# Batch 0 of a blockwise causal attention in two query parts, with the MoE layer begun between them

## The chip, the cores and the metric

The kernel runs on one core of a Trainium2 chip. The metric is the device time of one execution in microseconds (us), as a median over runs. Engine names: PE is TensorE (matmuls; PEld its weight loads), DVE is VectorE, ACT is ScalarE, POOL is GpSimd, SP is SyncE, which only issues DMAs here.

## The reference: what is computed

Attention over 8 batches, 8 heads, 576 positions and a head dimension of 64, with a mask that is causal by blocks of 64, followed by a maxout layer over all 4608 tokens.

```python
scores = scale * np.matmul(q, k.transpose(0, 1, 3, 2))        # (8, 8, 576, 576)
mask = block_i >= block_j                                     # blocks of 64
scores = np.where(mask, scores, -1000000000.0)
scores = scores - np.max(scores, axis=-1, keepdims=True)
attn = np.exp(scores)
attn = attn / (np.sum(attn, axis=-1, keepdims=True) + 1e-09)
attn_out = np.matmul(attn, v)
...
x = attn_out.transpose(0, 2, 1, 3).reshape(B * S, H * D)      # (4608, 512)
h1 = x @ w1                                                   # w1, w2: (512, 1024)
h2 = x @ w2
return np.maximum(h1, h2) @ w_out                             # w_out: (1024, 512)
```

All inputs and the output are float32; the kernel's matmuls take bf16.

## The kernel before, in words

The program is one straight stream for each engine; the order in which the Python code issues instructions is the order in which every engine runs its own, since the scheduler is set to manual. Waits between engines come from the tiles' dependencies.

**Attention.** Work goes by pairs of heads: 32 pairs (`p` or `s`), four to a batch, two to a group (`g`). A group's q and k come by DMA as float32 (`load_qk`, SP's queue, 576 KB each), are cast to bf16 (`cast`, on POOL, ACT or DVE), and turned on the PE by 18 small transposes each (`transposes`, L265), which ACT and DVE copy from PSUM to `qT` and `kT` (L272). `scores` (L282) makes the transposed scores of a pair: keys on partitions, queries along the free axis. They are issued in two bursts, `burst_a` and `burst_b`, through two PSUM buffers (`ps_s`); ACT's exponential (L288) writes them to `aT`: three of 1024 elements (512 columns of two heads) and one of 128. POOL's `mask` (L293) sets half blocks on the diagonal to zero. `av` (L333) multiplies with v, whose 65th column of ones gives the sum; 30 matmuls of 65 columns for a pair, for query tiles [0, 1] and [2, 3, 4]. DVE takes the reciprocal and multiplies (L339, L340) into `xp`; after a group, `x_out` turns it on the PE (18 small transposes) and DVE copies it into `xT` (L358, L359), the MoE layer's input with the model dimension on partitions. `done_tokens` is raised once both groups of a batch are there.

**MoE.** `h_unit(i, f)` takes one span of 512 tokens and one slice of 128 of the hidden dimension: 4 matmuls (L168) with w1, 4 with w2; DVE copies the first to bf16 (L175) and takes the maximum with the second (L177). `y_unit(i, s)` makes 128 rows of the output with 8 matmuls (L186), which ACT copies (L192) and SP stores. `y_last` does the last 128 rows in halves. Each matmul is one step of a generator, `moe()`; `needs` lists for each step how many tokens must be done; `ready()` counts the steps that may go, and `fill(n)` issues up to n of them at the place where it is called. `fill_of(s)` sets n: what is ready less 6, over the pairs left until the next batch is done.

**PSUM.** `ps_s` has two buffers of two banks; everything else on the PE takes one of four banks (`ps_m`).

**Order of the head.** `warm_up(n)` issues n matmuls on zeros (L254). q and k of the groups 0 to 2 are loaded at once, those of group 3 and 4 later (`pool_work`, each behind a small POOL memset that gates SP's DMA). POOL's queue also issues v (`load_v`, L109, five chunks for a batch), w1 and w2 (`load_w`, L120: columns 0 to 255, 256 to 511, then 512 to 1023) and w_out (`load_wo`, L123), all of them with a cast in the DMA; these use eight semaphores in turn, so that an issue waits for the landing of the one eight places earlier. After the four pairs of batch 0 come their `av`, the two `x_out`, and from there a loop over the pairs 4 to 31: a fill, `burst_a`, a fill, the transposes of a later group's q or k, `burst_b`, POOL's work, and the `av` of two pairs earlier with fills between. At pair 4 the transposes of group 2 (q and k) come first, between two fills of 6.

Of the kernel before, what the change touches and what calls it, by code (L numbers as in the profile page):

```python
# [14 lines left out]
def kernel(  # L15
# [38 lines left out]

    SPAN = 512
    NSPAN = NTOK // SPAN

# [31 lines left out]
    def load_qk(g, queues, gated=False):  # L89
        b, u = divmod(g, GPB)  # L90
        for nm, src, queue in (("q", q, queues[0]), ("k", k, queues[1])):
            raws[nm, g] = t = raw.tile([P, 2, RPP * D], FP32, name=f"{nm}raw")
            if gated:
                nc.gpsimd.memset(t[:, 0, :1], 0.0)
            queue.dma_start(
                out=t[:],
                in_=src[b, 4 * u:4 * u + 4].rearrange(
                    "(s h) (p t) d -> (h p) s (t d)", h=2, t=RPP),
            )
# [35 lines left out]
    load_qk(2, (SP, SP))  # L135
# [9 lines left out]
    cast("q", 0, ((dve, 0, 6), (pool, 6, RPP)))  # L145
# [3 lines left out]
    cast("q", 1, ((pool, 0, RPP),))  # L149
    for c in range(3, NCH):  # L150
        load_v(0, c)
    load_w(0, 256)
    load_w(256, 256)
# [5 lines left out]
    def h_unit(i, f):  # L159
# [3 lines left out]
        t0 = i * SPAN  # L163
        ph = []
        for w_sb in (w1_sb, w2_sb):
            pt = ps_m.tile([P, SPAN], FP32, name="ps_h", tag="m")
            for c in range(NDM):
                nc.tensor.matmul(  # L168
                    pt[:], w_sb[:, c, f * P:(f + 1) * P], xT[:, c, t0:t0 + SPAN],
                    start=(c == 0), stop=(c == NDM - 1),  # L170
                )
                if c == NDM - 1:
                    if not ph:
                        h1 = h1_pool.tile([P, SPAN], BF16, name="h1")
                        nc.vector.tensor_copy(out=h1[:], in_=pt[:])  # L175
                    else:
                        nc.vector.tensor_max(g[:, f, :], h1[:], pt[:])  # L177
# [3 lines left out]
    def y_unit(i, s):  # L181
        g = g_tiles[i]
        t0 = i * SPAN + s * P
# [12 lines left out]
    def y_last(i, s):  # L196
        g = g_tiles[i]
        t0 = i * SPAN + s * P
# [17 lines left out]
    def moe():  # L216
        ny = SPAN // P
        for i in range(NSPAN):
            need = (i + 1) * SPAN
            for f in range(NFF):  # L220
                yield from ((need, 0) for _ in h_unit(i, f))
                if i > 1 and f % 2 == 0:
                    yield from ((need, 0) for _ in y_unit(i - 1, f // 2))
            if i == 0:
                for s in range(ny):
                    yield from ((need, 0) for _ in y_unit(0, s))
        for s in range(ny - 1):
            yield from ((NTOK, 0) for _ in y_unit(NSPAN - 1, s))
        yield from ((NTOK, 0) for _ in y_last(NSPAN - 1, ny - 1))


    needs = []
    for i in range(NSPAN):
        needs += [(i + 1) * SPAN] * (2 * NDM * NFF + (SPAN // P * NFF if i != 1 else 0))
    needs += [NTOK] * ((SPAN // P + 1) * NFF)
    moe_steps = moe()
    at = [0]

    def ready():
        n = at[0]  # L240
        while n < len(needs) and needs[n] <= done_tokens[0]:
            n += 1
        return n - at[0]

    def fill(n):
        for _ in range(min(n, ready())):
            next(moe_steps)
# [44 lines left out]
    def mask(p, a0):  # L292
        nc.gpsimd.memset(aT_r[p % NA][BLK:, :, a0:a0 + BLK], 0.0)  # L293
# [23 lines left out]
    def av(p, ts):  # L317
# [11 lines left out]
        for gi, t in enumerate(ts):  # L329
            for hh in range(2):  # L330
                for c in range(t + 1):
                    a0 = CB[c] + t * P
# [12 lines left out]
    def x_out(g):  # L345
        b, u = divmod(g, GPB)
        xp = xps.pop(g)
        pe = ps_m.tile([P, 2, NCH, BLK], BF16, name="ps_xe", tag="m")
        po = ps_m.tile([P, 2, NCH - 1, BLK], BF16, name="ps_xo", tag="m")
        for s in range(2):  # L350
            for t in range(NCH):
                src = xp[:, t, s].rearrange("p a d -> p (a d)")
                nc.tensor.transpose(pe[:, s, t, :], src[:BLK], ident[:BLK, :BLK])  # L353
                if t < NCH - 1:
                    nc.tensor.transpose(po[:, s, t, :], src[BLK:], ident[BLK:, BLK:])
        dst = xT[:, 2 * u:2 * u + 2, b * S:b * S + NCH * P].rearrange(
            "p s (t h w) -> p s t h w", h=2, w=BLK)
        nc.vector.tensor_copy(out=dst[:, :, :, 0], in_=pe[:])  # L358
        nc.vector.tensor_copy(out=dst[:, :, :NCH - 1, 1], in_=po[:])  # L359
        if u == GPB - 1:  # L360
            done_tokens[0] = (b + 1) * S
# [13 lines left out]
    def pool_work(s):  # L375
        g, i = divmod(s, 2)
        if s == 0:
            load_w(512, 512)
            load_qk(3, (SP, SP), gated=True)
        elif s == 1 or s == 2:  # L380
            pass
        elif s == 3:
            cast("q", 2, ((act, 0, RPP),))
# [146 lines left out]
```

The softmax here doesn't subtract the row's maximum and nothing guards it: scores larger than these inputs give would overflow.

## Time and profile before

| | |
|---|---|
| median of 7 runs | 294.15 us (293.81 to 296.1) |
| profiled execution | 294.15 us, span from first to last instruction 292.4 us |
| granted PE clock | 1.00 |
| PE busy | 277.1 us, of which MoE h 133.6, MoE y 66.5 |
| DVE, ACT, POOL busy | 182.2, 140.1, 95.1 us |
| matmuls on zeros | 34 recorded, 10.9 us busy |
| first MoE matmul | recorded at 27.2 us, the following four at 28.19 |
| first scores of pair 4 and pair 5 | 32.14 and 36.75 us |
| exponentials of batch 0 | 9.32 to 22.5 us |

How to read it: times are from the start of the span; a row of the timeline gives start, length, engine, line, operation, output and inputs, and in brackets the idle time just before and what ended it. Matmuls overlap in their pipeline: a single one of 512 columns lasts 379 ns, and in a stream one starts every 217 ns (92 in 20 us between 240 and 260 us). A row "x4" is several instructions merged from the first start to the last end. The landing of a DMA is counted from its issue.

### The profile page before, as it was taken

What the parts mean: (1) busy time and instruction counts of PE and PEld (TensorE: products, weight loads), DVE (VectorE), ACT (ScalarE), POOL (GpSimd) and SP (SyncE); (2) the same over time, 40 slices, a digit from 0 to 9 for tenths busy, and PEclk for the clock granted to TensorE, in tenths of its full rate; (3) what the DMA queues carried; (4) which work ended last, traced back from release to release, by engine and by line L of the source; (5) the groups of instructions that cost most, each with busy time, mean ns of one, the idle gap of its engine ahead of it and who ended that gap; (6) DMA issues with size and microseconds to landing.
All of it is one profiled execution on the core that took longest, in us unless ns stands there. A gap on an engine that the chain in (4) does not pass through costs nothing.

```text
span 292.4 us, 7406 instructions
## 1 busy us (share of the span) xinstructions
PE 277.1 (95%) x3067; PEld 141.1 (48%) x3116; DVE 182.2 (62%) x363; ACT 140.1 (48%) x200; POOL 95.1 (33%) x236
## 2 busy tenths in 40 slices
PE   8787999999999999999999999999999999999995
PEld 3345445445554454544554455454545544444443
DVE  6717677547987676666565666666665766464530
ACT  3883687686655555554545555545555000101112
POOL 3958336625644443144324432443111000000000
PEclk9999999999999999999999999999999999999999
DMA  7999998959923792668656684455110111011104
GB/s 269 284 206 285 218 183 163 234 139 178 201 25 149 91 218 45 201 73 203 80 200 72 167 117 151 73 63 66 40 38 37 38 67 43 36 72 38 72 36 144
DMA packets 56081, 36.65 MB, mean 125 GB/s; under 512 B 38768, under 2 KB 43376, under 8 KB 56048
## 3 DMA queue, kind: packets, MB, share of 16 engines
q0 software_dynamic: 41728, 7.87, 33.6%
q1 hardware_dynamic: 13760, 27.60, 27.7%
q10 hardware_dynamic: 560, 0.72, 0.7%
q8 instruction: 24, 0.39, 0.6%
q14 instruction: 9, 0.07, 0.1%
HBM read 34.60 MB, written 9.44 MB: 151 GB/s over the span
## 4 chain that ended last, share of the span: by engine, by line
PE 90%; ACT 4%; DVE 3%; issue 2%; ACTq 0%
PE ps_h L168 42%; PE ps_y L186 20%; PE ps_o L333 11%; PE ps_s L282 8%; ACT aT L288 3%; PE ps_w L254 3%; PE ps_qT L265 2%; PE ps_kT L265 2%; PE ps_xe L353 2%; DVE xp L340 1%; PE ps_y L203 1%; DVE kT L272 1%; DVE xT L358 0%; DVE qT L272 0%; DVE rec L339 0%
## 5 line engine op out<-in xcount | busy, mean ns | idle before, releaser
L168 PE MATMUL ps_h<-xT,w_sb 128*128 128x512 bf16 x547 | 133.6, 379 | 3.5 <-issue 1.8
L288 ACT ACTIVATE aT<-ps_s 128x1024 bf16<-128x1024 f32 (+1 forms) x128 | 99.1, 832 | 53.6 <-PE ps_s L282 53.6
L168 PEld LDWEIGHTS <-w_sb 128*128 128x128 bf16 x576 | 51.9, 98 | 59.7 <-issue 6.1
L175 DVE CAST h<-ps_h 128x512 bf16<-128x512 f32 x72 | 49.7, 691 | 45.0 <-PE ps_h L168 43.8
L186 PE MATMUL ps_y<-wo_sb,g 128*128 128x512 bf16 x262 | 66.5, 379 | 1.0 <-issue 0.2
L293 POOL MEMSET aT<- 64x128 bf16 x128 | 23.5, 199 | 123.0 <-ACT aT L288 122.8
L192 ACT COPY y<-ps_y 128x512 f32<-128x512 f32 x35 | 20.5, 586 | 83.9 <-PE ps_y L186 56.8
L177 DVE TENSOR_TENSOR g<-h,ps_h 128x512 bf16<-128x512 bf16 x72 | 49.3, 684 | 10.2 <-PE ps_h L168 10.2
L333 PEld LDWEIGHTS <-aT 128*128 128x128 bf16 x960 | 33.6, 98 | 15.0 <-DVE xp L340 8.5
L333 PE MATMUL ps_o<-vv,aT 128*128 128x65 bf16 x960 | 39.7, 194 | 1.1 <-DVE xp L340 0.4
L186 PEld LDWEIGHTS <-g 128*128 128x128 bf16 x280 | 25.4, 98 | 27.9 <-issue 3.2
L282 PE MATMUL ps_s<-qT,kT 64*128 64x64 bf16 (+4 forms) x384 | 34.4, 275 | 3.3 <-ACT aT L288 3.2
L109 POOL DMA_DIRECT2D vv<-in_v_dram x40 | 33.7, 849 | 0.3 <-issue 0.3
L340 DVE TENSOR_TENSOR xp<-ps_o,rec 128x256 bf16<-128x256 f32 x64 | 31.4, 491 | 2.2
L282 PEld LDWEIGHTS <-kT 64*128 64x128 bf16 x384 | 16.5, 94 | 18.9 <-issue 13.1
L339 DVE RECIPROCAL rec<-ps_o 128x4 f32<-128x4 f32 x64 | 11.8, 184 | 18.9 <-PE ps_o L333 18.8
L105 POOL CAST qn<-qraw 128x1152 bf16<-128x1152 f32 (+1 forms) x15 | 16.7, 1111 | 4.3 <-DMA qraw<-in_q_dram 4.3
L272 DVE COPY qT<-ps_qT 128x576 bf16<-128x576 bf16 x17 | 12.8, 757 | 5.8 <-PE ps_qT L265 4.5
L358 DVE COPY xT<-ps_xe 128x640 bf16<-128x640 bf16 x16 | 7.8, 490 | 12.4 <-PE ps_xe L353 12.1
L272 DVE COPY kT<-ps_kT 128x576 bf16<-128x576 bf16 x17 | 12.8, 756 | 4.3 <-PE ps_kT L265 3.3
L105 POOL CAST kn<-kraw 128x1152 bf16<-128x1152 f32 x13 | 14.9, 1146 | 0.8
L254 PE MATMUL ps_w<-zeros 128*128 128x512 bf16 x34 | 10.9, 454 | 1.8 <-DVE zeros L132 1.2
(39 smaller groups left out, 103.3 us busy)
## 6 DMA issues: line engine op xcount, KB each, us to landing
qraw<-in_q_dram SPq DMA_DIRECT2D x16, 576.0 KB, 4.5
out_dram<-y SPq DMA_DIRECT2D x35, 256.0 KB, 2.1
kraw<-in_k_dram SPq DMA_DIRECT2D x15, 576.0 KB, 5.6
vv<-in_v_dram POOLq DMA_DIRECT2D x32, 128.0 KB, 5.8
w_sb<-in_moe_w_dram POOLq DMA_DIRECT2D x4, 256.0 KB, 9.0
w_sb<-in_moe_w_dram POOLq DMA_DIRECT2D x2, 512.0 KB, 16.8
wo_sb<-in_moe_w_out_dram POOLq DMA_DIRECT2D x2, 512.0 KB, 12.7
kraw<-in_k_dram ACTq DMA_DIRECT2D x1, 576.0 KB, 5.3
```

The costliest lines, as they stand in the source:

```text
L105: copy(out=n[:, j0:j1], in_=t[:, j0:j1])
L109: nc.gpsimd.dma_start(out=vv_r[b % NV][:rows, c, :, :D], in_=v[b, :, c * P:c * P + rows, :].rearrange("h p d -> p h d"),)
L168: nc.tensor.matmul(pt[:], w_sb[:, c, f * P:(f + 1) * P], xT[:, c, t0:t0 + SPAN], start=(c == 0), stop=(c == NDM - 1),)
L175: nc.vector.tensor_copy(out=h1[:], in_=pt[:])
L177: nc.vector.tensor_max(g[:, f, :], h1[:], pt[:])
L186: nc.tensor.matmul(py[:], g[:, f, s * P:(s + 1) * P], wo_sb[:, f, :], start=(f == 0), stop=(f == NFF - 1),)
L272: copies[i](out=t[:, :S].rearrange("q (p j) -> q p j", j=RPP), in_=pts[i].rearrange("q j p -> q p j"),)
L282: nc.tensor.matmul(ps[:m, hh, col:col + w], kT[r, c * P:c * P + m], qT[r, q0:q0 + w], start=True, stop=True,)
L288: nc.scalar.activation(out=aT_r[p % NA][:m, :, a0:a0 + w], in_=ps[:m, :, :w], func=AF.Exp, scale=scale,)
L293: nc.gpsimd.memset(aT_r[p % NA][BLK:, :, a0:a0 + BLK], 0.0)
L333: nc.tensor.matmul(po[:, gi, hh, :], a[:, hh, a0:a0 + P], vv[:, c, h0 + 2 * hh, :], start=(mm == 0), stop=(mm == n_mm - 1),)
L340: nc.vector.tensor_mul(xp[:, ts[0]:ts[0] + n, :, p % 2], po[:, :, :, :D], rec[:, :n].to_broadcast([P, n, 2, D]),)
```

## The change

Batch 0's queries are cut at position 384. For the four pairs of batch 0 the scores of the first 384 queries come first, in bursts of 512 and 256 columns (`burst_p1`, `burst_p2`); then those of the last 192, in bursts of 512 and 320 (`burst_q1`, `burst_q2`). So the four exponentials of a pair have 1024, 512, 1024 and 640 elements. `a_col` finds a block's place in `aT` for these pairs. `av` is called for the query tiles [0, 1, 2] and [3, 4], `x_out` for the tiles 0 to 2 and 3 to 4; `done_tokens` becomes 384 after the first part of group 1.

The first MoE span of 512 tokens becomes two, of 384 and 128. `fill` and `ready` count cost in place of steps: a step of 384 columns is 0.75, one of 128 is 0.25. The y units of spans 0 and 1 follow the h units of span 1.

In the head: q0's cast is split 7 to 2 between DVE and POOL; q1 is cast by DVE and k1 by POOL (before, the other way round). k2's load is issued later, behind a POOL memset that follows the first `load_w`. The masks of pairs 2 and 3 in the first part go to DVE. The first `load_w` comes behind pair 0's masks and ahead of v's chunks 3 and 4. q2 and k2 are cast by POOL in place of ACT, and their transposes come within batch 0, with all four copies on DVE. The casts of q3 and k3 on POOL stand behind both issues of w_out, before they stood between v's chunks 2 and 3 of batch 1. The matmuls on zeros are 37 (before 36), at other places. The first two `fill`s of 6 at pair 4 are gone; 17 steps of the 384-token span are issued before the loop, and the `av` for the tiles 3 and 4 of the pairs 2 and 3 in the loop at pair 4.

```diff
+    QCUT = 384
+    def a_col(p, c, t):
+        if p >= HP:
+            return CB[c] + t * P
+        return {
+            0: (0, 768 - QCUT), 1: (512 - P, 960 - QCUT),
+            2: (384 - 2 * P, 1152 - QCUT), 3: (0, 1344 - QCUT), 4: (0, 1536 - 4 * P),
+        }[c][t * P >= QCUT] + t * P if (c, t) != (2, 4) else 1280
     SPAN = 512
-    NSPAN = NTOK // SPAN
+    spans = [(0, QCUT), (QCUT, SPAN - QCUT)]
+    spans += [(t0, SPAN) for t0 in range(SPAN, NTOK, SPAN)]
+    NSPAN = len(spans)
...
-    load_qk(2, (SP, SP))
+    load_qk(2, (SP, None))
...
-    cast("q", 0, ((dve, 0, 6), (pool, 6, RPP)))
+    cast("q", 0, ((dve, 0, 7), (pool, 7, RPP)))
     cast("k", 0, ((act, 0, 5), (dve, 5, RPP)))
     for c in range(3):
         load_v(0, c)
-    cast("q", 1, ((pool, 0, RPP),))
-    for c in range(3, NCH):
-        load_v(0, c)
-    load_w(0, 256)
-    load_w(256, 256)
+    cast("k", 1, ((pool, 0, RPP),))
...
-        t0 = i * SPAN
+        t0, w = spans[i]
...
-                    pt[:], w_sb[:, c, f * P:(f + 1) * P], xT[:, c, t0:t0 + SPAN],
+                    pt[:, :w], w_sb[:, c, f * P:(f + 1) * P], xT[:, c, t0:t0 + w],
...
+    def plan():
+        def h(i, f):
+            t0, w = spans[i]
+            units.append((h_unit(i, f), t0 + w, w / SPAN, 2 * NDM))
+        def y(i, s, last=False):
+            t0, w = spans[i]
+            if last:
+                units.append((y_last(i, s), t0 + w, 0.5, 2 * NFF))
+            else:
+                units.append((y_unit(i, s), t0 + w, 1.0, NFF))
         for i in range(NSPAN):
-            need = (i + 1) * SPAN
             for f in range(NFF):
-                yield from ((need, 0) for _ in h_unit(i, f))
-                if i > 1 and f % 2 == 0:
-                    yield from ((need, 0) for _ in y_unit(i - 1, f // 2))
-            if i == 0:
-                for s in range(ny):
-                    yield from ((need, 0) for _ in y_unit(0, s))
-        for s in range(ny - 1):
-            yield from ((NTOK, 0) for _ in y_unit(NSPAN - 1, s))
-        yield from ((NTOK, 0) for _ in y_last(NSPAN - 1, ny - 1))
-    needs = []
-    for i in range(NSPAN):
-        needs += [(i + 1) * SPAN] * (2 * NDM * NFF + (SPAN // P * NFF if i != 1 else 0))
-    needs += [NTOK] * ((SPAN // P + 1) * NFF)
-    moe_steps = moe()
+                h(i, f)
+                if i > 2 and f % 2 == 0:
+                    y(i - 1, f // 2)
+            if i == 1:
+                for j in range(2):
+                    for s in range(spans[j][1] // P):
+                        y(j, s)
+        n = spans[-1][1] // P
+        for s in range(n):
+            y(NSPAN - 1, s, s == n - 1)
+    plan()
...
+        n, total = at[0], 0.0
+        while n < len(steps) and steps[n][1] <= done_tokens[0]:
+            total += steps[n][2]
             n += 1
-        return n - at[0]
+        return int(total)
     def fill(n):
-        for _ in range(min(n, ready())):
-            next(moe_steps)
+        while n > 0 and at[0] < len(steps) and steps[at[0]][1] <= done_tokens[0]:
+            u, _, cost = steps[at[0]]
+            next(u)
+            n -= cost
...
+    def burst(p, parts, a0):
+        u = ps_s.tile([P, 2, 512], FP32, name="ps_s", tag="s")
+        w = 0
+        for c, q0, n in parts:
+            scores(p, u, w, c, q0, n)
+            w += n
+        exp(p, u, w, a0)
+    def burst_p1(p):
+        burst(p, ((0, 0, QCUT), (2, 256, P)), 0)
+    def burst_p2(p):
+        burst(p, ((1, P, QCUT - P),), 512)
+    def burst_q1(p):
+        burst(p, ((0, QCUT, 192), (1, QCUT, 192), (2, QCUT, P)), 768)
+    def burst_q2(p):
+        burst(p, ((2, 512, BLK), (3, QCUT, 192), (4, 512, BLK)), 1280)
+    def masks_p(p, eng=None):
+        for a in (0, 384, 512):
+            mask(p, a, eng)
+    def mask_q(p, eng=None):
+        mask(p, 1344, eng)
...
-                    a0 = CB[c] + t * P
+                    a0 = a_col(p, c, t)
...
-            done_tokens[0] = (b + 1) * S
+            done_tokens[0] = min(b * S + t1 * P, (b + 1) * S)
...
-        if s == 0:
-            load_w(512, 512)
-            load_qk(3, (SP, SP), gated=True)
-        elif s == 1 or s == 2:
-            pass
-        elif s == 3:
-            cast("q", 2, ((act, 0, RPP),))
-            cast("k", 2, ((act, 0, RPP),))
-            load_qk(4, (SP, SP), gated=True)
-            for c in range(3):
-                load_v(1, c)
-            cast("q", 3, ((pool, 0, RPP),))
-            cast("k", 3, ((pool, 0, RPP),))
-            for c in range(3, NCH):
-                load_v(1, c)
-            load_wo(0, 4)
-            load_wo(4, 4)
-        elif s == 4:
+        if s == 4:
...
-    for s in range(HP):
-        burst_a(s)
-        if s == 0:
-            cast("k", 1, ((dve, 0, RPP),))
-            warm_up(4)
-        elif s == 1:
-            transposes("k", 1, (dve, dve))()
-            warm_up(2)
-        elif s == 2:
-            av(0, [0, 1])
-            warm_up(2)
-        else:
-            av(0, [2, 3, 4])
-        burst_b(s)
-        pool_work(s)
-        if s == 0:
-            transposes("q", 1, (dve, dve))()
-            warm_up(2)
-        elif s == 1:
-            warm_up(4)
-        elif s == 2:
-            warm_up(3)
-    for p in (1, 2, 3):
-        av(p, [0, 1])
-        av(p, [2, 3, 4])
-        if p == 2:
-            x_out(0)
-    x_out(1)
+    cast("q", 1, ((dve, 0, RPP),))
+    burst_p1(0)
+    burst_p2(0)
+    warm_up(2)
+    masks_p(0)
+    load_w(0, 256)
+    load_qk(2, (None, SP), gated=True)
+    cq = transposes("q", 1, (dve, dve))
+    burst_p1(1)
+    ck = transposes("k", 1, (dve, dve))
+    for i in range(2):
+        cq((i,))
+        ck((i,))
+    burst_p2(1)
+    masks_p(1)
+    for c in range(3, NCH):
+        load_v(0, c)
+    warm_up(2)
+    burst_p1(2)
+    warm_up(2)
+    av(0, [0, 1, 2])
+    burst_p2(2)
+    masks_p(2, nc.vector)
+    load_w(256, 256)
+    warm_up(3)
+    burst_p1(3)
+    av(1, [0, 1, 2])
+    warm_up(2)
+    burst_p2(3)
+    masks_p(3, nc.vector)
+    load_w(512, 512)
+    load_qk(3, (SP, SP), gated=True)
+    cast("q", 2, ((pool, 0, RPP),))
+    cast("k", 2, ((pool, 0, RPP),))
+    burst_q1(0)
+    av(2, [0, 1, 2])
+    warm_up(2)
+    burst_q2(0)
+    av(3, [0, 1, 2])
+    x_out(0, 0, 3)
+    burst_q1(1)
+    warm_up(2)
+    burst_q2(1)
+    mask_q(0)
+    mask_q(1)
+    for c in range(3):
+        load_v(1, c)
+    warm_up(3)
+    burst_q1(2)
+    x_out(1, 0, 3)
+    fill(4)
+    burst_q2(2)
+    mask_q(2)
+    fill(2)
+    burst_q1(3)
+    av(0, [3, 4])
+    fill(3)
+    burst_q2(3)
+    cq = transposes("q", 2, (dve, dve))
+    ck = transposes("k", 2, (dve, dve))
+    for i in range(2):
+        cq((i,))
+        ck((i,))
+    mask_q(3)
+    for c in range(3, NCH):
+        load_v(1, c)
+    load_wo(0, 4)
+    load_wo(4, 4)
+    load_qk(4, (SP, SP), gated=True)
+    cast("q", 3, ((pool, 0, RPP),))
+    cast("k", 3, ((pool, 0, RPP),))
+    av(1, [3, 4])
+    fill(3)
+    x_out(0, 3, NCH)
     x_due = []
     for s in range(HP, NPAIR):
         g, i = divmod(s, 2)
         if x_due:
-            x_out(x_due.pop())
+            x_out(x_due.pop(), 3 if s == HP + 1 else 0)
         n = fill_of(s)
-        if s == HP:
-            fill(6)
-            cq = transposes("q", 2, (dve, act))
-            ck = transposes("k", 2, (dve, act))
-            cq()
-            ck()
-            fill(6)
         burst_a(s)
         n_a = n // 2 if n > 12 else n * 2 // 5
         n_b = n // 6
...
             av(p, [2, 3, 4])
             if p % 2:
                 x_due.append(p // 2)
+        elif s == HP:
+            av(2, [3, 4])
+            fill(n_b)
+            av(3, [3, 4])
+            x_due.append(1)
```

The lines left out hand the widths to the other MoE operations, put `x_out`'s tile range into its slices, build `steps` from `plan()` in place of `moe()`, and rename `needs`.

## The prediction

> **What bounds the kernel now.** I read the page first (busy shares, groups), then the busy time by stage, then TensorE's timeline, then ScalarE, GpSimd and the DMA issues of the stage that the change touches.
>
> ```profile
> PE 277.1 (95%) x3067; PEld 141.1 (48%) x3116; DVE 182.2 (62%) x363; ACT 140.1 (48%) x200; POOL 95.1 (33%) x236
> L168 PE MATMUL ps_h<-xT,w_sb 128*128 128x512 bf16 x547 | 133.6, 379 | 3.5 <-issue 1.8
> ```
>
> TensorE is busy for 95% of the span, and of the idle time almost none lies before MoE matmuls. But the share counts the matmuls on zeros (L254), and it is an average. By stage:
>
> ```profile
> 6.94:28.19 21.25, 16.13 (x296) 9.93 (x300) 12.49 (x28) 15.26 (x20) 16.70 (x38) 1.00 1.47 259
> 28.19:36.75 8.56, 7.86 (x90) 3.52 (x92) 5.64 (x9) 4.89 (x7) 3.80 (x9) 1.00 1.73 227
> ```
>
> (Columns: length, then busy time of PE, PEld, DVE, ACT, POOL, then clock, DMA share, GB/s.) The first row is batch 0: from the end of the first zeros to the first MoE unit.
>
> ```profile
> 17.29 0.40 PE L282 MATMUL ps_s<-qT,kT 64*128 64x320 bf16 x4 [0.17 <-ACT aT L288]
> 18.20 0.21 PE L282 MATMUL ps_s<-qT,kT 64*128 64x64 bf16 x2 [0.52 <-ACT aT L288]
> 18.34 0.82 PE L254 MATMUL ps_w<-zeros 128*128 128x512 bf16 x3
> ...
> 21.68 2.00 PE L333 MATMUL ps_o<-vv,aT 128*128 128x65 bf16 x60
> ...
> 28.19 1.02 PE L168 MATMUL ps_h<-xT,w_sb 128*128 128x512 bf16 x4 [0.59 <-DVE xT L359]
> ...
> 36.75 0.61 PE L282 MATMUL ps_s<-qT,kT 64*128 64x512 bf16 x6
> ```
>
> Until 21.5 us the PE waits for ScalarE's exponentials and fills the waits with zeros; from 21.7 to 28.2 it waits for VectorE's chain of normalising and copying. From 28.19 on MoE work fills it. The useful work in these 21.25 us is: 120 attention-value matmuls at 0.031 (60 in 2.00, less one latency of 0.19), 3.7 us; four pairs' scores at 0.54 + 0.31 (the two bursts of one pair in the chain of waits), 3.4; 72 + 36 small transposes at 0.0145 (18 in 0.26), 1.6. That is 8.7 us, so **12.5 us is the most** that MoE work brought forward could win. After 28.19 the PE does the same work as before the change, so the question is only how much of it is done at a given time.
>
> **The walk of the head.** Durations: an exponential of 1024 elements takes 1.02 us, of 128 elements 0.26, so by a line through both 0.59 for 512 and 0.70 for 640, each 0.1 less when back to back.
>
> ```profile
> 9.32 3.00 ACT L288 ACTIVATE aT<-ps_s 128x1024 bf16<-128x1024 f32 x4 [0.51 <-PE ps_s L282]
> ```
>
> Per pair the old four (3.00 in this row) become 0.92 + 0.49 for the first query part and 0.92 + 0.60 for the second, 2.93 in all: ScalarE's work stays. With no gap it would end at 9.4 + 11.7 = 21.1.
>
> 1. Start. VectorE casts 7 instead of 6 rows of q0 (+0.1 us), so the first exponential starts at 9.40 instead of 9.32. q1's cast (1.35 us) goes to VectorE behind two copies (ends 10.2), k1's to GpSimd behind v's three issues (9.0 to 10.2); q1's and k1's four copies follow on VectorE at 0.71 each (row 11.80, 1.42 for two): 11.3, 12.0, 12.7, 13.4. Pair 2 needs the second of them, at 12.0, when ScalarE still has work until 12.4. Hidden.
> 2. First value matmuls. Pair 0's stand on the PE at 12.85 and need v's third chunk. Before, they came at 16.3 and later, and that chunk (issue 7.8) took:
>
> ```profile
> vv<-in_v_dram POOLq DMA_DIRECT2D x1, 128.0 KB, 7.3
> ```
>
> That is 15.1 us. The DMA view shows no software packet from 6 to 10 us while q and k run at 403 GB/s; they come at full rate (1.2 per ns) from 11.5, when those end. k2 (0.59 MB, 1.5 us) now stays behind, so I shift the landing by 1.5, to 13.6; the bounds are 13.0 and 15.1. Cost: the PE stalls 0.75 us (0.2 to 2.3), ScalarE 0.3.
> 3. The first part's exponentials end at 16.6, the second's first one runs from 16.6. Pair 2's and 3's masks are on VectorE (3 x 0.11 per pair, row of L144), and VectorE has finished the four normalisings (0.70 each for 6 columns) at 18.7 and pair group 0's and 1's transposed copies (0.33 each, by the rows of 0.49 for 640 and 0.41 for 512) at 21.1. So **MoE starts at 20.5 instead of 28.2**, its second half of contraction steps at 21.15. Its weights were issued at 11.2 (before 11.4, landed 7.3 later): hidden by 1.8 us or more.
> 4. The rest of part 2 runs in PE order: 17 steps of 384 columns at 0.163 (0.217 x 3/4) between the bursts, the last exponential ends at 25.1. Then q2's and k2's transposes: four copies on VectorE, and the PE tiles are four, so k2's second half waits for q2's first copy (the row of before shows the like: 0.6 us of ps_kT behind qT). Copies end at 25.5, 26.7, 27.4, 28.1; pair 1's last value matmuls, their normalising (28.7) and the last transposes follow, and pair 4's first burst is issued at 29.0, against 32.14.
> 5. GpSimd meanwhile: last mask at 25.2, two v issues 1.58, first wo issue 0.77, to 27.7. The second wo issue reuses the semaphore of w1's second half and so waits for its landing L; then casts of q3 and k3. Before, these casts stood ahead of wo:
>
> ```profile
> 28.17 1.58 POOL L109 DMA_DIRECT2D vv<-in_v_dram  x2
> 29.71 1.54 POOL L123 DMA_DIRECT2D wo_sb<-in_moe_w_out_dram  x2
> ```
>
> q3's transposes on the PE come at 30.0; q3's cast ends at L + 0.77 + 0.1 + 1.15. w1's half is issued at 16.4 (before 15.0) and took
>
> ```profile
> w_sb<-in_moe_w_dram POOLq DMA_DIRECT2D x1, 512.0 KB, 15.2
> ```
>
> So L is 31.6 at most by that row. Less, because half its time it shared the engines with q3, k3, q4 (software bytes 0.18 to 0.25 MB per 2 us beside them, 0.39 alone, 18 to 20 us), and q4 now goes out only behind wo. With k2 in 16.4 to 19.2 and q3, k3 in 21.5 to 27.1, the software bytes reach its end at 26.4 and it lands at **L = 28** (27 to 31.6). The cast then ends at 30.0, just in time.
> 6. Pair 4's second burst, the last 36 value matmuls of batch 0 (1.1), 4 steps (0.65), the last transposes: pair 5's first burst at 32.95, where the row above has 36.75.
>
> **Sum.** Lead at that burst 36.75 - 32.95 = 3.80 us. MoE steps done by then, in steps of 512 columns: before 27 (6 + 6 + 15, from the fill rule: 90 left over 6), after 24 x 0.75 = 18. Owed 9 x 0.217 = 1.95. The 128-token span: by rows its matmul lies on the line from 0.031 (65 columns) to 0.217, at 0.058, so 64 cost 3.7 against 3.5; but VectorE's 16 casts and maxima on 128 elements take 0.28 each (the row of a 128-element copy says 0.29) beside normalising and copying, 5.8 us for pair 7's turn where the PE has 5.4: 0.4 lost. 3.80 - 1.95 - 0.40 = 1.45. From batch 2 on nothing differs. The profiled execution took 294.15 us (span 292.4 and 1.75 around it), which is also the median of the seven runs: 294.15 - 1.45 = **292.7 us**.
>
> Two rules of the Trainium skill speak against this. Its page "TensorE: Matmul & The Clock Gate", section "Back-to-back issue gap", gives about 81 ns for a sustained matmul of 128 columns: 64 of them would cost 1.7 us over the quarter of 512 columns, and the sum would be 294.2; the trace's 65-column rows of 31 ns speak for the smaller price. Its page "DMA: Bandwidth & Descriptors", section "Queues, rings and completion order", says that each engine goes round the queues packet by packet; then k2's absence would bring v little, the landing would stay at 15.1, and the sum would be about 293.9. The empty software queue from 6 to 10 us speaks against that.
>
> **Rivals.**
> - *The head runs closer to ScalarE's bound.* The walk ends ScalarE's part at 25.1, 4.0 past the bound of 21.1, by waits in PE order that I placed by hand. If half of them are not there, 2 us more: 290.7. For it: two score buffers, as before, where the waits were 1.5 us over batch 0. Against it: the PE order now has transposes and values between the bursts.
> - *The lead is eaten.* v at 15.1, or L near 29.5: 1 to 1.5 us lost, 293.3 to 295.0. The change then does what it says and shows nothing.
> - *Slower: GpSimd's queue.* Each us of L beyond 28 delays q3's cast, the PE stands at q3's transposes, and everything is behind it. At 31.6 it costs 3.6: 296.3; at before's own landing, 30.2, 294.9. Beyond L = 30.4 the kernel is slower by over 0.3%; I put the case at 295.6. For it: the same row's 15.2 us. Against it: q4 is out of the way.
>
> **How the numbers follow.** Forecast 0.42, closer to the bound 0.19, lead eaten 0.19, GpSimd's queue 0.20. Faster by over 0.3% (0.9 us, about what a measurement of this kernel can tell from no change), below 293.3: the second case whole and most of the first, 0.56; within: 0.23; slower: 0.21. The range reaches from 289.7 (the second case, less 1) to 295.7 (the middle of the last).
>
> **What would show it.** After's timeline: the first MoE matmul (20.5 forecast), the first score burst of pair 5 (32.95), a PE wait at the first value matmuls for v (0.75), and at q3's transposes for GpSimd's cast (none; 3.6 in the last rival); the second wo issue against 28. The forecast is wrong if ScalarE's exponentials of batch 0 end more than 1 us from 25.1, or if pairs 5 to 9 take over 29.6 us (26.7 before, plus 9 x 0.217 and 0.4 is 29.1).

## The result, and the profile after

The changed kernel takes **295.54 us** as a median of 13 runs (294.95 to 297.77), the kernel before, on the same chip, 294.02 us (34 runs): a ratio of 1.0052, 95% interval 1.0036 to 1.0069. The forecast was 292.7, faster; it is slower by half a per cent. The profiled execution took 295.81 us, span 294.0.

The page of after, its shares and its clock by slice:

```profile
PE 279.9 (95%) x3160; PEld 145.3 (49%) x3205; DVE 186.3 (63%) x391; ACT 137.7 (47%) x196; POOL 96.3 (33%) x233
...
PEclk9998899999999999999999999999999999999999
```

The shares say as little as before did. The line to look at is PEclk, the granted clock of TensorE in tenths: two slices of 8, where before had none. The busy time by stage of after (length, busy time of PE, PEld, DVE, ACT, POOL, clock, DMA share, GB/s), first from the end of the first zeros to the first MoE matmul, then to pair 5's first burst:

```profile
6.94:20.95 14.01, 12.31 (x216) 6.63 (x220) 10.06 (x25) 10.77 (x16) 13.00 (x26) 1.00 1.54 235
20.95:35.00 14.05, 11.84 (x198) 7.00 (x193) 9.68 (x23) 6.93 (x9) 9.12 (x17) 0.88 1.58 224
```

The first stage does what was forecast: MoE's first matmuls stand at 20.95 us, where before had them at 27.2 and 28.2, and the change does what it says. The second has 2.2 us of idle PE and a mean clock of 0.88. TensorE's timeline of after there (start, length, then in brackets the idle time before and what ended it):

```profile
26.36 0.42 PE L291 MATMUL ps_kT<-ident,kn 64*128 64x64 bf16 x17 [0.62 <-DVE qT L298]
27.62 1.01 PE L386 MATMUL ps_o<-vv,aT 128*128 128x65 bf16 x18 [0.84 <-DVE kT L298]
28.44 1.47 PE L181 MATMUL ps_h<-xT,w_sb 128*128 128x384 bf16 x4
...
30.05 1.04 PE L308 MATMUL ps_s<-qT,kT 64*128 64x512 bf16 x5
...
31.87 0.44 PE L291 MATMUL ps_qT<-ident,qn 64*128 64x64 bf16 x18
...
32.78 0.21 PE L308 MATMUL ps_s<-qT,kT 64*128 64x64 bf16 x2 [0.26 <-ACT aT L314]
...
35.05 0.59 PE L308 MATMUL ps_s<-qT,kT 64*128 64x512 bf16 x5
```

Two waits at the copies of q2 and k2; then the same four matmuls of 384 columns that took 0.81 us at 24 us take 1.47, and five of 512 columns take 1.04 where the last row's take 0.59. That is the clock, in the stages of 2 us:

```profile
26.00:28.00 2.00, 0.80 (x27) 0.77 (x27) 1.50 (x3) 0.00 (x0) 1.90 (x4) 0.96 1.15 282
28.00:30.00 2.00, 2.00 (x23) 1.04 (x21) 1.78 (x5) 0.00 (x0) 0.82 (x2) 0.50 1.30 205
30.00:32.00 2.00, 1.91 (x25) 0.80 (x22) 0.80 (x4) 1.21 (x2) 1.96 (x5) 0.69 2.28 160
```

The granted clock was halved for 3.41 us, from 27.84 to 31.25 (a mean of 0.96 leaves 0.16 us at one half ahead of 28.00, one of 0.69 leaves 1.25 behind 30.00). GpSimd's timeline of after at the same time:

```profile
27.84 0.78 POOL L140 DMA_DIRECT2D wo_sb<-in_moe_w_out_dram  x1
29.80 0.74 POOL L140 DMA_DIRECT2D wo_sb<-in_moe_w_out_dram  x1 [1.18 <-DMA w_sb<-in_moe_w_dram]
...
30.66 1.15 POOL L122 CAST qn<-qraw 128x1152 bf16<-128x1152 f32 x1
```

The second issue of w_out (some of the recorded expectations below call w_out w2) waits until w1's second half has landed, L = 29.8, and q3's cast ends at 31.81; q3's transposes start 0.06 later. The PE, at half clock until 31.25, comes to them at 31.77, so its wait for the cast is only 0.1 here. So pair 4's first burst comes at 29.95, pair 5's at 35.00 and pair 10's at 64.86; before they came at 32.14, 36.75 and 63.42. A lead of 2.2 us has become a debt of 1.44 by pair 10. From there both kernels do the same, and the debt stays to the end (1.66 between the two profiled executions). Pair 10's first burst in before, then in after:

```profile
63.42 0.38 PE L282 MATMUL ps_s<-qT,kT 64*128 64x512 bf16 x1
```

```profile
64.86 0.38 PE L308 MATMUL ps_s<-qT,kT 64*128 64x512 bf16 x1
```

### The profile page after: what moved, and what is told of

Read it like the earlier page. It is cut to its first block, busy times and chain, and to the rows that moved or that the text cites. A ratio compares the mean times of both kernels' runs of the same rounds, so it can differ in the third digit from the quotient of the medians.

```text
span 294.0 us, 7606 instructions
## 1 busy us (share of the span) xinstructions
PE 279.9 (95%) x3160; PEld 145.3 (49%) x3205; DVE 186.3 (63%) x391; ACT 137.7 (47%) x196; POOL 96.3 (33%) x233
## 4 chain that ended last, share of the span: by engine, by line
PE 87%; DVE 4%; DMA 4%; issue 2%; ACT 1%; POOL 1%; DVEq 0%; ACTq 0%
PE ps_h L181 41%; PE ps_y L199 20%; PE ps_o L386 12%; PE ps_s L308 8%; DMA vv<-in_v_dram 2%; PE ps_xe L408 2%; DMA qraw<-in_q_dram 2%; PE ps_kT L291 2%; PE ps_qT L291 2%; DVE xp L393 1%; PE ps_w L280 1%; ACT aT L314 1%; DVE g L190 1%; DVE kT L298 1%; POOL vv L126 1%
## 5 line engine op out<-in xcount | busy, mean ns | idle before, releaser
L181 PE MATMUL ps_h<-xT,w_sb 128*128 128x512 bf16 (+2 forms) x616 | 136.8, 359 | 3.5 <-issue 1.6
L314 ACT ACTIVATE aT<-ps_s 128x1024 bf16<-128x1024 f32 (+3 forms) x128 | 100.1, 832 | 63.0 <-PE ps_s L308 56.1
L181 PEld LDWEIGHTS <-w_sb 128*128 128x128 bf16 x640 | 56.0, 98 | 60.0 <-issue 7.4
L188 DVE CAST h<-ps_h 128x512 bf16<-128x512 f32 (+2 forms) x80 | 50.9, 636 | 45.1 <-PE ps_h L181 43.6
L205 ACT COPY y<-ps_y 128x512 f32<-128x512 f32 x35 | 20.5, 586 | 83.7 <-PE ps_y L199 56.6
L190 DVE TENSOR_TENSOR g<-h,ps_h 128x512 bf16<-128x512 bf16 (+2 forms) x80 | 50.5, 631 | 10.3 <-PE ps_h L181 9.3
L308 PE MATMUL ps_s<-qT,kT 64*128 64x64 bf16 (+6 forms) x408 | 35.2, 271 | 0.6 <-DVE kT L298 0.3
L393 DVE TENSOR_TENSOR xp<-ps_o,rec 128x256 bf16<-128x256 f32 (+1 forms) x64 | 31.4, 491 | 2.2
L308 PEld LDWEIGHTS <-kT 64*128 64x128 bf16 x408 | 16.5, 95 | 14.9 <-issue 9.7
L392 DVE RECIPROCAL rec<-ps_o 128x4 f32<-128x4 f32 (+1 forms) x64 | 11.8, 185 | 15.8 <-PE ps_o L386 15.7
L122 POOL CAST qn<-qraw 128x1152 bf16<-128x1152 f32 (+1 forms) x15 | 16.5, 1101 | 4.6 <-DMA qraw<-in_q_dram 4.6
L122 POOL CAST kn<-kraw 128x1152 bf16<-128x1152 f32 x15 | 17.2, 1145 | 1.0 <-DMA kraw<-in_k_dram 0.3
L298 DVE COPY qT<-ps_qT 128x576 bf16<-128x576 bf16 x18 | 13.6, 757 | 4.8 <-PE ps_qT L291 3.8
L298 DVE COPY kT<-ps_kT 128x576 bf16<-128x576 bf16 x18 | 13.6, 756 | 4.6 <-PE ps_kT L291 3.4
L413 DVE COPY xT<-ps_xe 128x640 bf16<-128x640 bf16 (+2 forms) x18 | 8.2, 453 | 13.1 <-PE ps_xe L408 11.4
```

What stands on the lines that cost most here:

```text
L122: copy(out=n[:, j0:j1], in_=t[:, j0:j1])
L181: nc.tensor.matmul(pt[:, :w], w_sb[:, c, f * P:(f + 1) * P], xT[:, c, t0:t0 + w], start=(c == 0), stop=(c == NDM - 1),)
L188: nc.vector.tensor_copy(out=h1[:, :w], in_=pt[:, :w])
L190: nc.vector.tensor_max(g[:, f, :w], h1[:, :w], pt[:, :w])
L298: copies[i](out=t[:, :S].rearrange("q (p j) -> q p j", j=RPP), in_=pts[i].rearrange("q j p -> q p j"),)
L308: nc.tensor.matmul(ps[:m, hh, col:col + w], kT[r, c * P:c * P + m], qT[r, q0:q0 + w], start=True, stop=True,)
```

## The experiments

Theory A: the sum was right in kind, and single waits ate the lead: GpSimd's queue ahead of q3's cast, the chain of copies of q2 and k2, and the narrow span. Rival B: the halved clock did it. Rival C: the lead is bound by something that no order cures (ScalarE, the transfers), and the debt of 9 MoE steps then decides. All edits are to the changed kernel; the kernel before ran beside each group (294.32, 294.43, 294.37 and 294.68 us).

**e1: casts of q3 and k3 ahead of w_out's issues.**

```diff
+    cast("q", 3, ((pool, 0, RPP),))
+    cast("k", 3, ((pool, 0, RPP),))
     load_wo(0, 4)
     load_wo(4, 4)
     load_qk(4, (SP, SP), gated=True)
-    cast("q", 3, ((pool, 0, RPP),))
-    cast("k", 3, ((pool, 0, RPP),))
```

> The casts of q3 and k3 stand ahead of the two w_out issues in GpSimd's queue; nothing else differs from the changed kernel (295.5 us, profile 294.0 us of span). Theory queue (the second w_out issue, held until 29.80 us by the landing of w1's second half, delays q3's cast to 31.81 and the PE stands for it) alone: the cast ends near 29.1, q3's transposes move from 31.87 to 30.3, the time falls by 1.5 to 294.0. Theory clock (the PE ran at half clock from 27.84 to 31.25 us and is late by itself): the transposes still come at 31.6, and the time falls by no more than 0.3, to 295.2.

Measured: 296.12 us (295.29 to 298.24), ratio 1.0067 [1.0044, 1.0089]. The clock was full through the head. TensorE's timeline of e1:

```profile
30.71 0.44 PE L291 MATMUL ps_qT<-ident,qn 64*128 64x64 bf16 x18
...
32.08 0.21 PE L308 MATMUL ps_s<-qT,kT 64*128 64x64 bf16 x2 [0.52 <-ACT aT L314]
...
42.53 0.44 PE L291 MATMUL ps_qT<-ident,qn 64*128 64x64 bf16 x18 [1.06 <-POOL qn L122]
```

The wait for q3's cast is gone, and two others stand in its place. Pair 4's second burst now waits 0.52 for ScalarE, so pair 5 comes at 34.30, 0.7 earlier than in after. And the load of q4, now behind everything on GpSimd, lands at 41.3; the PE waits 1.06 for its cast, and pair 10's burst comes at 65.28. Neither forecast came (294.0 and 295.2): what the order gave at one place it took at another.

**e7: matmuls on zeros in the two waits of the copies**, into a score buffer; **e4: the same with e1's order.**

```diff
+    def warm_s(n):
+        pw = ps_s.tile([P, 2, 512], FP32, name="ps_ws", tag="s")
+        for _ in range(n):
+            nc.tensor.matmul(pw[:, 0, :], zeros[:, :P], zeros[:], start=True, stop=True)
...
     cq = transposes("q", 2, (dve, dve))
+    warm_s(3)
     ck = transposes("k", 2, (dve, dve))
+    warm_s(4)
```

> The changed kernel with 3 matmuls on zeros between q2's and k2's transposes and 4 behind k2's, where the PE stood idle for 0.62 and 0.84 us; they go to a score buffer that is free then. Theory clock alone: the clock stays at 1.00, the PE does 1.6 us more work by 31.3, the time falls by 1.4 to 294.1. Theory queue: q3's transposes still wait for the cast at 31.8, now with a wait of about 1.5 us on the PE, and the time stays within 0.2 of 295.5.

> Both edits of the two runs before it. If queue and clock hide behind one another, each alone gives little and both give 1.5 to 1.8: 293.9, with pair 5's first burst at 33.4 instead of 35.0. If one of them is the whole cause, this run equals the run of that one alone.

Measured: e7 295.75 us (294.94 to 298.9), 1.0073 [1.0043, 1.0104]; e4 295.8 (295.44 to 297.93), 1.0057 [1.0037, 1.0078]. In e4's profiled execution the clock is full through the head and nothing is won: pair 5 at 34.32, and again a wait for q4's cast (0.41). e7's profiled execution is one of its longest, 298.65 us, and so shows what a late landing does. GpSimd and TensorE in e7:

```profile
31.77 0.74 POOL L140 DMA_DIRECT2D wo_sb<-in_moe_w_out_dram  x1 [1.80 <-DMA w_sb<-in_moe_w_dram]
```

```profile
33.83 0.60 PE L297 MATMUL ps_qT<-ident,qn 64*128 64x64 bf16 x18 [2.74 <-POOL qn L122]
...
34.85 2.16 PE L392 MATMUL ps_o<-vv,aT 128*128 128x65 bf16 x36
```

L is 31.8, the PE stands 2.74 us at q3's transposes, and after that wait the clock is halved (36 value matmuls take 2.16 instead of 1.27). Pair 5 comes at 37.90. Here the halved clock follows a stall of the queue (it stands from 33.92, and the wait ends at 33.83): in such an execution B is a consequence of A.

**e5: the narrow span's units mixed with output units.**

```diff
                 h(i, f)
+                if i == 1 and f in (1, 3, 5):
+                    y(0, f // 2)
...
-                for j in range(2):
-                    for s in range(spans[j][1] // P):
-                        y(j, s)
+                y(1, 0)
```

> The changed kernel with the y units of the 384-token span put behind every second h unit of the 128-token span, instead of behind all of them. Theory narrow span (VectorE's casts and maxima on 128 columns run one after another at 0.29 us while the PE needs 0.25 for the 4 matmuls between them; PE idle 1.0 us between 48 and 56 us): 0.7 less, 294.8. Theory that the idle time is ScalarE's and only moves to the y units: within 0.2 of 295.5.

Measured: 295.26 us (294.12 to 298.58), 1.0036 [1.0003, 1.0069]. Up to pair 5 it is the changed kernel, at full clock in the profiled execution: pair 4 at 29.53, q3's transposes wait 1.00 for the cast, pair 5 at 34.47. From pair 5 to pair 10 it takes 29.11 us, after 29.86. After's timeline of that stretch shows what went:

```profile
48.64 0.42 PE L291 MATMUL ps_kT<-ident,kn 64*128 64x64 bf16 x17 [0.19 <-DVE g L190]
...
49.90 0.38 PE L181 MATMUL ps_h<-xT,w_sb 128*128 128x128 bf16 x4 [0.19 <-DVE kT L298]
50.45 0.29 PE L181 MATMUL ps_h<-xT,w_sb 128*128 128x128 bf16 x2 [0.17 <-DVE xp L393]
...
52.42 0.73 PE L181 MATMUL ps_h<-xT,w_sb 128*128 128x128 bf16 x10 [0.32 <-DVE xp L393]
```

Units of 128 columns run off faster than VectorE empties them; an output unit between them lets it keep up. 0.75 us of the narrow span's price is order, not work. The median falls less than forecast (294.8), as the list falls in two: six executions at a mean clock of 0.998 or more took 294.12 to 295.32, median 294.2 and so level with the kernel before (294.32); six at 0.994 took 295.20 to 298.58.

**e8: e5 with half of the copies of q2 and k2 on ScalarE; e9: e8 with the casts of q3 and k3 and the load of q4 ahead of w_out's issues.** The first four lines of the edit, with e5's, are e8; e9 adds the rest.

```diff
-    cq = transposes("q", 2, (dve, dve))
-    ck = transposes("k", 2, (dve, dve))
+    cq = transposes("q", 2, (dve, act))
+    ck = transposes("k", 2, (dve, act))
...
+    cast("q", 3, ((pool, 0, RPP),))
+    load_qk(4, (SP, SP), gated=True)
+    cast("k", 3, ((pool, 0, RPP),))
     load_wo(0, 4)
     load_wo(4, 4)
-    load_qk(4, (SP, SP), gated=True)
-    cast("q", 3, ((pool, 0, RPP),))
-    cast("k", 3, ((pool, 0, RPP),))
```

> The interleaved kernel (295.26 us; its profile 292.5 us of span), with the second of the two copies of q2's and of k2's transposes on ScalarE, which stands idle from 26.0 to 30.1 us, instead of VectorE. Theory copy chain (four copies in a row on VectorE set the time of pair 4's first burst, 29.53 us): that burst comes at 28.5. Theory queue: q3's transposes still wait for the cast, which ends at 31.7, so that pair 5's first burst stays at 34.4 and the time within 0.2 of the interleaved kernel. If the queue hides nothing, 1.0 less: 294.2.

> The run before it with q3's cast, then the loads of q4 and k4, then k3's cast ahead of the two w_out issues. In the run with the casts alone ahead, q4's load was issued at 32.5 instead of 30.7, landed at 41.3 and the PE stood 1.06 us for its cast; here it is issued at 29.1. Theory chain and queue together: q3's transposes at 29.8, pair 5's first burst at 33.2 instead of 34.47, 1.2 less than the interleaved kernel by profile: a span of 291.3, under before's 292.4. If the transfers are the bound (everything that is loaded earlier makes something else land later), w_out or v of batch 1 lands late and the span stays at 292.5.

Measured: e8 295.72 us (295.44 to 297.52), 1.0058 [1.0037, 1.008]; e9 294.26 (292.88 to 295.28), 0.9996 [0.9981, 1.001]. In e8 pair 4 comes at 28.34, 1.6 earlier than in after, and all of it and more is lost at the cast, pair 5 coming at 35.75:

```profile
31.70 0.66 PE L291 MATMUL ps_qT<-ident,qn 64*128 64x64 bf16 x18 [2.12 <-POOL qn L122]
...
32.77 2.16 PE L386 MATMUL ps_o<-vv,aT 128*128 128x65 bf16 x36
```

The clock is halved behind the wait once more. In e9, without that wait, pair 5 is at 32.98 (the forecast's 32.95) and pair 10 at 62.17; the profiled execution is its shortest, 292.88 us. The other eleven, at clocks of 0.999 to 1.000, took 293.5 to 295.3: something else was still late in them.

**e10: k2's load at the start again; e11: e9 with the same.**

```diff
-    load_qk(2, (SP, None))
+    load_qk(2, (SP, SP))
...
-    load_qk(2, (None, SP), gated=True)
```

> The changed kernel with k2 loaded at the start, as before the change. Theory of step 2 (k2 behind lets v land 1.5 us earlier): v's third chunk lands at 15.1 instead of 13.77, the PE waits 1.7 us for it instead of 0.43, the exponentials of batch 0 end 1.0 later, and the time rises by 0.8, to 296.3. Rival (k2's late landing, 5.7 to 8.6 us after its issue in five profiles, holds up GpSimd's queue in some executions and makes the times spread): the slow end of the spread goes, and the median falls to 295.2 or less.

> Interleaved y units, copies on ScalarE, casts and q4's load ahead of w_out, and k2 loaded at the start. By the theory of step 2 it is 0.8 slower than the same without k2's load at the start; by the rival it is faster than that by 0.3 and spreads less.

Measured: e10 297.76 us (296.75 to 297.96), 1.0106 [1.0088, 1.0123]; e11 295.67 (294.27 to 297.13), 1.0037 [1.0016, 1.0059]. v's third chunk in after and in e10:

```profile
13.77 0.28 PE L386 MATMUL ps_o<-vv,aT 128*128 128x65 bf16 x4 [0.43 <-DMA vv<-in_v_dram]
```

```profile
14.34 0.31 PE L386 MATMUL ps_o<-vv,aT 128*128 128x65 bf16 x5 [0.82 <-DMA vv<-in_v_dram]
15.22 0.28 PE L386 MATMUL ps_o<-vv,aT 128*128 128x65 bf16 x4 [0.57 <-DMA vv<-in_v_dram]
```

Holding k2 back brings v 1.45 us earlier, as step 2 of the prediction had it (1.5). Without it pair 4 comes at 32.29, and the median is 2.2 us longer than after's, where 0.8 was forecast. But that isn't v alone: in e10's trace the clock is halved within batch 0, from 16.3 to 19.7 us, and five of its six executions have a mean clock of 0.992 to 0.994; the one at full clock took 296.75. In e11 the four executions at full clock (median 294.43) are level with e9's 294.26, so there v's delay costs nothing that shows. e11 also prices the clock: four of its executions have a mean clock of 1.000 and took 294.27 to 294.61 us, six have 0.993 or 0.994 (one halved window) and took 295.58 to 295.89, two have 0.987 and took 296.91 and 297.13. One window costs about 1.3 us in this kernel; in the trace it stands in batch 0, from 15.9 to 19.3.

**e13: e9 with all four copies on VectorE. e14 and e15: after and e9 once more, for the trace of a second execution.**

> The kernel of e9 without its ScalarE half of the copies of q2 and k2 (all four on VectorE again): later units between the narrow span's, the casts of q3 and k3 and the loads of q4 and k4 ahead of w2's two issues. If GpSimd's queue was the one thing in the way of the lead, pair 4 stays at 29.5 us, q3's transposes no longer wait, and pair 5's first burst comes within 0.5 us of e9's 32.98: a span of about 291.5, time level with e9's 294.3. If the chain of copies counts as well, pair 5 comes at 34 us or later and pair 10's burst at 63.2 or later: 295.0.

> The changed kernel once more, unedited, for the trace of a second execution. If the halved clock made the difference to the kernel before, an execution without the halved window has its pair 5 near 33.5 us and a time within 0.3 us of 294.2. If the queue of GpSimd and the narrow span made it, an execution at full clock still has pair 5 at 34.3 to 35.0 us, pair 10 at 64.0 to 64.9 and a time of 295.0 to 295.6; the halved window then costs nothing of its own, or a few tenths.

> The kernel of e9 once more, for the trace of a second execution: its executions at one clock spread over 292.9 to 295.3 us. If the spread comes from the landings at the start (v's, and w1's second half, which GpSimd's queue waits for), the lateness is there at pair 5's first burst (33.0 in the profiled one of 292.88 us), and the stretch from pair 10 to the end is the same to 0.3 us. If it comes from the body, pair 5 stays near 33.0 and the distance from pair 10 to the end differs.

Measured: e13 294.23 us (293.96 to 296.1), 0.9992 [0.9978, 1.0006]; e14 295.69 and e15 293.78 in one execution each. e14 repeats after: clock 0.994, L 29.5, pair 4 at 29.88, pair 5 at 34.93. As it caught a halved window, it doesn't tell what an execution at full clock does; after's own list does. Six of its executions have 0.998 or more and took 294.95 to 295.85, median 295.31; eight have 0.994, median 295.94. The two groups differ by 0.6 us; as a late landing can bring the window with it (e7), that is at most the window's own price. B leaves 1.3 us between the six and the kernel before unexplained. In e13 the four executions at 0.994 are only 0.2 us longer than the others. e13 has pair 4 at 29.72 and pair 5 at 34.49, as late as e5, though no cast is in the way; e9, with the same wait of 0.52 for ScalarE behind pair 4, has 28.22 and 32.98. So the copies count, as e13's second theory had it for the trace; its median is e9's nevertheless, as the first had it. The execution profiled in e13 took 296.10, and there and in e15 stands what can be late in e9. First e15's, then e13's timeline, at the first output unit:

```profile
47.93 0.59 PE L199 MATMUL ps_y<-wo_sb,g 128*128 128x512 bf16 x2 [0.76 <-DMA wo_sb<-in_moe_w_out_dram]
```

```profile
50.23 0.59 PE L199 MATMUL ps_y<-wo_sb,g 128*128 128x512 bf16 x2 [1.63 <-DMA wo_sb<-in_moe_w_out_dram]
```

Both edits of e9 made w_out's second half critical: its issue is later (31.1 to 31.9; in after 29.8), and the output unit that needs it is earlier (45.2; in after 54.6). It lands 15.9, 16.5 and 18.3 us after its issue in e9, e15 and e13, and the PE waits 0, 0.76 and 1.63. e15 is at 33.06 at pair 5, as e9 was, and at 63.06 at pair 10, 0.9 later; its time is 0.9 longer. That e13 and e9, 1.5 us apart at pair 5, have one median fits both standing at this landing; e16 puts that to the test.

**e16: e9 with w_out's issues ahead of k3's cast, and output units two units later.**

```diff
     load_qk(4, (SP, SP), gated=True)
-    cast("k", 3, ((pool, 0, RPP),))
     load_wo(0, 4)
     load_wo(4, 4)
+    cast("k", 3, ((pool, 0, RPP),))
...
-                if i == 1 and f in (1, 3, 5):
-                    y(0, f // 2)
+                if i == 1 and f in (3, 5, 7):
+                    y(0, f // 2 - 1)
```

> The kernel of e9 with w2's two issues ahead of k3's cast, and the first span's output units after the narrow units f = 3, 5, 7 instead of 1, 3, 5. In e9 and e13 the wait of the first output unit for w2's second half was 0 us in the execution of 292.88 us, 0.76 us in that of 293.78 and 1.63 us in that of 296.10. If that wait is what the executions differ by, it is gone in every one here: pair 5's first burst at 33.0, pair 10's at 62.2 to 62.5, a median of 292.9 to 293.3 us and a ratio to the kernel before of 0.995 to 0.997. If the executions differ by something else (the landing of v, q4 or k3, the clock), the median stays at 294.2 and pair 10's burst moves about as before.

Measured: **292.62 us (292.49 to 292.74, 6 runs)**, ratio 0.9932 [0.991, 0.9955], clocks 0.999 to 1.000. It beats both kernels, by a little more than forecast (292.9 to 293.3), and the spread of 2.4 us in e9 is down to 0.25. GpSimd and TensorE in e16:

```profile
27.95 1.14 POOL L122 CAST qn<-qraw 128x1152 bf16<-128x1152 f32 x1
...
31.44 0.74 POOL L140 DMA_DIRECT2D wo_sb<-in_moe_w_out_dram  x1 [1.58 <-DMA w_sb<-in_moe_w_dram]
32.18 1.16 POOL L122 CAST kn<-kraw 128x1152 bf16<-128x1152 f32 x1
```

```profile
29.68 0.44 PE L291 MATMUL ps_qT<-ident,qn 64*128 64x64 bf16 x18
...
33.32 0.59 PE L308 MATMUL ps_s<-qT,kT 64*128 64x512 bf16 x5
...
35.58 0.44 PE L291 MATMUL ps_kT<-ident,kn 64*128 64x64 bf16 x18
...
62.01 0.38 PE L308 MATMUL ps_s<-qT,kT 64*128 64x512 bf16 x1
```

The landing L is late here too, 31.4, and GpSimd waits 1.58 for it. But q3's cast is ahead of it, k3's ends at 33.3 for transposes at 35.58, and the PE waits neither for a cast nor for w_out (0.84 us for the copies of q2 and 0.52 for ScalarE are left). Pair 5 is at 33.27, pair 10 at 62.01. That is C's end: the lead can be had, and outweighs the debt.

## Why the prediction was wrong

The accounting at pair 10, where the two kernels are again at the same place in their work, in us of gain:

| | forecast | after | e16 |
|---|---|---|---|
| lead at pair 5's first burst (36.75 less its time) | 3.80 | 1.75 | 3.48 |
| 9 MoE steps owed | -1.95 | -1.95 | -1.95 |
| narrow span (what is left of pairs 5 to 9, 26.67 before) | -0.40 | -1.24 | -0.12 |
| sum; it is the difference of pair 10's bursts | 1.45 | -1.44 | 1.41 |

The debt was right: by pair 5's first burst the trace of before has 27 weight loads for MoE matmuls, those of after and e16 24 at three quarters of the columns, and by pair 10's all three have done the same 90 steps' worth. With the two other terms cured the sum stands. **The terms that failed are the lead and the price of the narrow span.** By the steps:

1. Start: right. The first exponential starts at 9.46 (9.40).
2. v: right. It lands at 13.77 (13.6), the wait is 0.43 (0.75); with k2 early it is 15.22, the forecast's upper bound of 15.1. The software packets come at full rate from 10 us in after, when the hardware queue is done (81 from 8 to 10 us beside 352 of the hardware queue, then 2412 beside 9); in e10 none come before 10, and 686 from 10 to 12. The prediction read the rule of the Trainium skill's page "DMA: Bandwidth & Descriptors", section "Queues, rings and completion order", as leaving v at 15.1; the landings speak against that reading here. Later in after the two queues do move about equal numbers of packets, as the page says (173 and 183 from 22 to 24 us). What holds the software packets back until 10 us isn't shown.
3. First MoE matmul: 20.95 (20.5). Right within half a us.
4. End of batch 0: the last exponential ends at 26.0 (25.1), within the bound that was set. Pair 4's first burst is at 29.53 in e5, which is the same program up to there at full clock: 0.53 late, by the chain of copies (with half of them on ScalarE, in e8, it is at 28.34). In after it is at 29.95; the other 0.42 is the halved clock, which no step had.
5. GpSimd's queue: mis-sized. L is 29.8 (28; the bounds were 27 and 31.6), so q3's cast ends at 31.8 and not "just in time" at 30.0. The rival named this as the slower end. Its price of 1 us for each us of L doesn't hold at this L: 1.8 late, it leaves a wait of 1.00 on the PE in e5 and 0.18 at pair 5 (step 6). In e7, at L = 31.8, it costs 2.74 us at the PE and a halved window besides.
6. Pair 4's second burst to pair 5: the walk gave 3.95 us from burst to burst. Where no cast is in the way it takes 4.76 (e1 and e9), 0.81 more. The walk names neither ScalarE's wait of 0.52 there nor a price for q3's own transposes (0.46); as it doesn't itemise the 3.95, how the 0.81 divides stays open. With the cast's wait of 1.00 in e5 it takes 4.94, so 0.18 of that wait is left when ScalarE's is behind it. After takes 5.05.

The lead's shortfall of 2.05 is thus 0.53 (copies) + 0.42 (clock) + 0.81 (walk of pair 4) + 0.18 (cast) + 0.11 (the rest of the halved window). That is for the profiled execution; where L is later, the cast's share grows, as e7 shows. Curing the queue alone (e1) gave nothing in the time, since ScalarE's wait and then q4's load came next. What the experiments show as the working cure is all of it together: copies on two engines, q3's cast and q4's load ahead of the wait for w1, w_out's need moved behind its landing, and output units between the narrow ones.

What sets L in one execution shows at the start of the traces, in the matmuls on zeros. After, then e16:

```profile
1.23 4.95 PE L280 MATMUL ps_w<-zeros 128*128 128x512 bf16 x16 [1.23 <-DVE zeros L149]
```

```profile
1.23 6.46 PE L280 MATMUL ps_w<-zeros 128*128 128x512 bf16 x16 [1.23 <-DVE zeros L149]
```

In after q0's transposes start at 7.00, when q0's cast is done; in e16 the cast is done at 6.87, but the zeros still run, and the transposes start at 7.63. The exponentials, the masks and so the first issue of w1 come later by as much (11.18 in after, 11.80 in e16). L is 29.5 to 29.8 in the four traces with those transposes at 6.80 to 7.00 (after, e14, e5, e8), and 31.4 and 31.8 in the two with 7.63 and 7.44 (e16, e7); up to there the six kernels are the same. How 0.6 us at the issue becomes nearly 2 at the landing isn't traced, and no run changed these zeros.

The narrow span's matmuls cost what was forecast: 10 of 128 columns took 0.73 from the first start to the last end (the row at 52.42), which less the 0.22 of a single one is 0.057 for each of the nine others (0.058 forecast). What failed is VectorE's part, named in the sum and taken at 0.40; e5 shows 0.75 of it to be order. The Trainium skill's page "TensorE: Matmul & The Clock Gate", section "Back-to-back issue gap", gives 81 ns for 128 columns; the trace shows less. The sign that was set for this, pairs 5 to 9 over 29.6 us, came with 29.86.

Of the rivals, B is a part: 0.5 us in the lead of the profiled execution and at most 0.6 in the medians, against a miss of 2.8. C fell with e16.

## What to carry to other kernels

A lead that is won early is worth only what comes through the next serial stage: list each engine's queue there, and ask of every instruction what it waits for and who stands behind it. An issue that can wait for a transfer belongs behind what the bottleneck needs next, and moving it makes its own transfer late, so look for its first reader as well. When one kernel's executions spread by several times the measurement's uncertainty at one clock, compare the traces of two of them: here that showed the transfer which the median hid, and that matmuls issued to fill the first wait can themselves hold up the first real ones.

## What the runs showed of the hardware

The granted clock fell to one half in single blocks of about 3.4 us: from 27.84 to 31.25 in after, 31.72 to 35.12 in e8, 33.92 to 37.36 in e7. In e8 and e7 the block came within 0.1 us of the end of waits of 2.12 and 2.74 us, in after 0.2 us behind the second of two waits of 0.62 and 0.84. The waits alone don't decide it: e1, e5 and e13 have the same two waits, with the PE busy for 0.84, 0.84 and 0.65 of the 2 us from 26 to 28 (0.80 in after, 0.96 in before), and kept the full clock. In e10 and e11 the block stands in batch 0.

Executions of a mean clock of 0.994 or less were 8 of 14 in after, 6 of 12 in e5, 5 of 12 in e7, 7 of 7 in e8, 5 of 6 in e10 and 8 of 12 in e11; 4 of 13 in e13, 1 of 10 in e1 and in e4, 0 of 12 in e9 and 0 of 6 in e16. So they are rare in the kernels without the cast's wait, but not in e10, whose trace has no such wait, nor in e11. What sets the block off isn't shown.

The landing of a transfer of 512 KB with a cast varied by about 2 us between the traces of kernels that are the same up to its issue: L from 29.5 to 31.8. Two executions of one kernel differ by less: L 29.8 and 29.5 in after and e14, and w_out's second half 15.9 and 16.5 us after its issue in e9 and e15.
